# A hand-ordered attention and maxout kernel: another order of the same units, nine evictions moved to ScalarE, one bias replaced by a mask product

## The chip, the cores and the metric

The kernel runs on one core of a Trainium2 chip. A core has TensorE (PE; its weight loads are listed as PEld), VectorE (DVE), ScalarE (ACT), GpSimd (POOL) and SyncE (SP), which issues DMA transfers. The engines run side by side; each works through its own instructions strictly in program order, and semaphores hold an instruction until its inputs are there and its output buffer is free. The metric is device time of one execution in microseconds (us).

## The reference

```python
def _attn_ref(q, k, v, n_global, n_local) -> np.ndarray:
    B, H, S, D = q.shape                      # 4, 8, 768, 64
    scale = 1.0 / np.sqrt(D)
    scores = scale * np.matmul(q, k.transpose(0, 1, 3, 2))
    ...
    is_global = pos[None, :] < int(n_global)                # 8
    is_local = (rel >= 0) & (rel < int(n_local))            # 96
    keep = is_global | is_local
    dist = np.where(is_global & ~is_local, float(n_local), np.abs(rel).astype(np.float32))
    slopes = 2.0 ** (-8.0 * (np.arange(H, dtype=np.float32) + 1) / H)
    bias = -slopes[:, None, None] * dist[None, :, :]
    scores = np.where(keep, scores + bias[None], -1000000000.0)
    ...
    return np.matmul(softmax(scores), v)
def _moe_ref(x, w1, w2, w3, w_out) -> np.ndarray:           # x: 3072 x 512, d_ff = 768
    h = np.maximum(np.maximum(x @ w1, x @ w2), x @ w3)
    return (h @ w_out).astype(np.float32)
```

The last two lines of the first function are shortened to their meaning. The attention output, heads side by side, is x: 3072 rows of 512.

## The kernel before

The 3072 rows are 24 tiles T0 to T23 of 128 rows, six to a batch. A tile attends to itself, to the tile before it and to 8 global keys, which are copied over unused places of the tile before. The tiles are grouped in seven chunks (SIZES, line 89: 4, 2, 2, 4, 4, 4, 4 tiles) for the maxout product, which is computed transposed: chunk c, slice f of 128 of the 768 hidden features, matrix j of three.

Nothing is scheduled by a tool: the string SCHEDULE (line 25) lists 782 units in one order, and each engine gets its instructions in that order. A unit is a letter, numbers, sometimes a last number that chooses the engine that does it (0 ScalarE, 1 VectorE, 2 GpSimd) and, behind @, the buffer slot that it writes. For x, F, O, t, S, A and b that slot is one of the eight banks of PSUM (S, b and A take two neighbouring ones), so a unit with @4 on TensorE waits until the last user of bank 4 has been read out. The units that matter here:

| unit | what it does | line |
|---|---|---|
| l, w, q | load of queries, keys, values (l0, l1, l2; 512 KB for two tiles), weights, output weights, from SP's queue | 229, 236, 514, 523 |
| c, v, W, Q | casts to bfloat16: queries and keys (c0, c1 . pair of tiles), values (v tile . half), weights (W group . matrix), output weights | 195/201, 254 |
| x, y, X | transposes of queries and keys on TensorE with a copy out of PSUM, or as a DMA transpose (X) | 270/276, 283/287, 292 |
| G, V | copies of the global keys and of the global rows of the values | 313/315, 323/325 |
| b, S | bias added to a score tile by an identity matmul; the scores (S tile . half . 1 on top of a bias, 0 alone) | 335, 349 |
| e, m | exp on ScalarE; product with the mask of distances, needed only where no bias was added | 356, 365/367 |
| B, K | the bias and the mask, per head, made once at the start | 373, 378 |
| A, n | product with the values; division by the sum, into xb | 391/394, 402/403 |
| t, u, Z | transpose of xb to xT on TensorE with a copy, or as a DMA transpose (Z) | 418, 421, 424 |
| F, f | maxout product F c.f.j; f ...0 copies the first matrix's tile out of PSUM, f ...1 and f ...2 are maxes with the next two | 433, 447/449/452 |
| O, o, s | output product of one row tile; its copy; its store | 457, 471, 478 |
| E | the output products of the last three tiles of the last chunk but one piece | 457, 462, 463 |
| D | matmuls on zeros at the start | 532 |

Chunks 0, 1 and 2 and tile 11 get xT by t and u; the other tiles by Z. A cast by GpSimd (line 201) is two instructions, one by ScalarE or VectorE (line 195) one.

```python
    def u_c(slot, a, G, p, how):
        ...
        cast(how, dst, raw[a, G, p].rearrange("i (j s) (e d) -> i j e s d", s=2, e=2))
    def u_m(slot, T, g, how):
        if biased[T, g]:
            return
    ...
        for u in todo[:2] + [None] + todo[2:]:
            if u is None:
                setup()
                continue
            code, _, slot = u.partition("@")
            units[code[0]](int(slot) if slot else None, *(int(n) for n in code[1:].split(".") if n))
```

Of the kernel before, what the change touches and what calls it, by code (L numbers as in the profile page):

```python
# [34 lines left out]
    F0.2.0@5 f0.4.0.1@1 F0.1.0@6 v4.1.2 v4.0.2 l2.3.2@0 f0.1.0.0@2 q2@0 v5.1.0 F0.0.0@0 F0.5.1@1 F0.4.1@4  # L35
    F0.2.1@6 m4.0.1 f0.0.0.0@3 v5.0.0 f0.5.0.0@4 m5.1.1 A4@2 V4.1.0 F0.3.1@0 W0.1.2 f0.4.1.1 W0.2.0 m5.0.1
    f0.5.1.1 F0.0.1@1 F0.1.1@4 V4.0.1 W1.2.0 n4@1 t4@7 A5@2 W2.2.0 c1.3.2.2@0 f0.0.1.1 f0.1.1.1 F0.1.2@1
    n5@0 u4.1@1 f0.1.2.1@0 F0.0.2@4 q0@1 t5@7 u5.0 q1@2 f0.3.1.1 f0.0.2.1 F0.2.2@2 F0.3.2@3 f0.3.2.1
    c0.3.2.0 f0.2.0.0@2 f0.2.1.1 F1.2.0@4 F1.0.2@7 Q2.0 v7.1.2 F1.0.0@5 f1.0.0.1@3 v6.1.2 F1.0.1@3 f0.2.2.1
    f1.0.1.1 f1.2.0.1@0 Q0.2 f1.0.2.1@1 x3.1.2@6 y3.1.2.1@3 F0.4.2@5 f0.4.2.1 l1.4.2@3 v6.0.2 Q1.2 F1.1.0@0  # L40
    F1.2.2@1 l0.4.2@4 l1.6.2@5 F1.2.1@4 f1.2.1.1 F1.3.1@2 f1.2.2.1 F1.3.2@3 v7.0.2 F1.3.0@4 f1.3.0.0@2
    f1.3.1.1 f1.3.2.1 x3.0.2@1 F0.5.2@5 f0.5.2.1 F1.4.0@2 F1.1.1@3 f1.1.0.0@3 y3.0.2.0 S6.0.0@0 S6.1.0@4
    G6.2 c1.4.2.2@1 c0.4.2.2 l0.5.2@0 c0.5.2.2@2 f1.1.1.1 f1.4.0.0@1 e6.0@4 S7.0.0@6 S7.1.0@2 l1.5.2@6
    c1.5.2.2 e6.1@5 c1.6.2.2@0 e7.1@6 F1.4.1@0 e7.0@7 l2.4.2@1 O0.2@1 f1.4.1.1 m7.1.1 x4.1.2@0 F1.5.2@2
    F1.5.0@3 m7.0.1 v8.1.2 F1.5.1@4 A7@6 f1.5.0.1@0 m6.1.1 m6.0.1 o0.2.0@0 y4.1.2.0@0 f1.5.1.1 f1.5.2.1
    x4.0.2@3 y4.0.2.0 G7.0 l0.6.2@1 c0.6.2.2 F1.4.2@5 O0.1@4 f1.4.2.1 n7@2 o0.1.1@1 A6@0 l2.5.2@2 S8.1.0@2
    S8.0.0@6 n6@3 V7.1.1 G8.1 v8.0.2 F1.1.2@4 O0.3@5 t6@0 v11.0.2 v9.0.2 v9.1.2 f1.1.2.1 V7.0.0 t7@1 e8.1@0
# [564 lines left out]
```

## Time and profile before

| | us |
|---|---|
| median of 3 runs | 175.62 (174.99 to 176.35) |
| the profiled execution | 176.69 |
| its span, first to last instruction | 174.8 |
| DMA: bytes moved, mean rate | 37.36 MB, 214 GB/s |

One execution was recorded by the hardware profiler. A busy time is the time in which an engine had at least one instruction under way. "Idle before" is the time that an engine stood still before an instruction, with what released it. The chain of waits is followed back from the last instruction: at each step to what released it, or to the instruction before it on its engine. PEclk is the clock that TensorE was granted, 1.00 being full.

### The profile page before, as it was taken

To read this page: it belongs to the slowest core of one execution; us is meant where nothing else is said; L and a number is where in the kernel's file an instruction comes from. 1 tells how busy PE (TensorE), PEld (TensorE's weight loads), DVE (VectorE), ACT (ScalarE), POOL (GpSimd) and SP (SyncE) were. 2 spreads that over 40 slices of the span, in tenths; PEclk is the share of its full clock that TensorE was granted. 3 is DMA by queue.
4 is the path that set the end of the run, shared out by engine and by line. 5 is a ranking of instruction groups with operands and counts; after the bars stand their busy time and mean duration, and the time that the engine had idled before them with its cause. 6 is when DMAs were issued, how large, how long until landed. Compare 5 with 4: busy or idle time off the path is not lost.

```text
span 174.8 us, 3865 instructions
## 1 busy us (share of the span) xinstructions
PE 165.9 (95%) x1485; PEld 93.6 (54%) x1507; DVE 131.9 (75%) x268; ACT 95.4 (55%) x147; POOL 54.7 (31%) x99
## 2 busy tenths in 40 slices
PE   7997999999999999898999999999999999999991
PEld 2555745577676877544445545544445554444460
DVE  7889864988599897989898678899578993074910
ACT  5988897672868788440667688200345651402051
POOL 4049295057586717003730003240530000000000
PEclk9999999999999999999999999999999999999998
DMA  5999999999899899999996759998990046370035
GB/s 149 352 292 327 402 360 385 270 371 311 229 303 179 139 183 266 267 290 284 165 135 112 114 145 306 305 210 260 231 213 20 0 120 137 121 286 4 0 119 185
DMA packets 66403, 37.36 MB, mean 214 GB/s; under 512 B 24144, under 2 KB 61392, under 8 KB 66384
## 3 DMA queue, kind: packets, MB, share of 16 engines
q1 hardware_dynamic: 66240, 37.04, 83.3%
q8 instruction: 12, 0.20, 0.5%
q10 hardware_dynamic: 144, 0.07, 0.1%
q14 instruction: 7, 0.06, 0.1%
HBM read 25.17 MB, written 6.29 MB: 180 GB/s over the span
## 4 chain that ended last, share of the span: by engine, by line
PE 76%; DVE 10%; DMA 6%; ACT 3%; issue 2%; SPq 0%; DVEq 0%
PE psum L433 44%; PE psum L457 17%; PE psum L349 6%; DMA xT<-xb 3%; DMA rawqk<-in_k_dram 3%; DVE P L365 3%; PE psum L391 3%; PE psum L394 2%; PE psum L276 2%; DVE ht L452 1%; DVE xb L403 1%; ACT P L356 1%; PE psum L270 1%; DVE qb L195 1%; PE psum L335 1%
## 5 line engine op out<-in xcount | busy, mean ns | idle before, releaser
L433 PE MATMUL psum<-xT,w 128*128 128x512 bf16 (+1 forms) x491 | 97.5, 348 | 1.5 <-DMA xT<-xb 0.7
L433 PEld LDWEIGHTS <-w 128*128 128x128 bf16 x504 | 47.6, 98 | 42.9 <-DMA xT<-xb 0.9
L356 ACT ACTIVATE P<-psum 128x1024 bf16<-128x1024 f32 (+1 forms) x48 | 43.3, 954 | 10.4 <-PE psum L349 10.3
L449 DVE TENSOR_TENSOR h<-h,psum 128x512 bf16<-128x512 bf16 (+1 forms) x42 | 25.0, 605 | 15.9 <-PE psum L433 12.4
L457 PE MATMUL psum<-wo,ht 128*128 128x512 bf16 (+2 forms) x147 | 33.4, 362 | 0.5
L447 ACT CAST h<-psum 128x512 bf16<-128x512 f32 (+1 forms) x27 | 13.8, 523 | 33.1 <-PE psum L433 29.8
L452 DVE TENSOR_TENSOR ht<-h,psum 128x512 bf16<-128x512 bf16 (+1 forms) x42 | 26.2, 644 | 2.1 <-PE psum L433 0.9
L365 DVE TENSOR_TENSOR P<-P,wmask 128x1024 bf16<-128x1024 bf16 x34 | 25.2, 752 | 2.0 <-ACT P L356 1.7
L457 PEld LDWEIGHTS <-ht 128*128 128x128 bf16 x156 | 13.8, 98 | 13.5 <-DVE ht L452 0.2
L254 POOL CAST va<-rawv 64x512 bf16<-64x512 f32 x28 | 18.5, 668 | 4.8 <-DMA rawv<-in_v_dram 3.7
L323 POOL COPY va<-vaf 4x260 int32<-4x260 int32 x17 | 7.2, 424 | 34.9 <-PE psum L394 34.5
L403 DVE TENSOR_TENSOR xb<-psum,rz 128x512 bf16<-128x512 f32 x24 | 16.6, 692 | 0.8
L201 POOL CAST qb<-rawk 128x512 bf16<-128x512 f32 x12 | 7.5, 654 | 23.7 <-DMA rawk<-in_k_dram 23.7
L349 PE MATMUL psum<-qkT 64*128 64x128 bf16 x352 | 14.4, 217 | 0.5 <-DVE qkT L315 0.4
L391 PEld LDWEIGHTS <-P 128*128 128x128 bf16 x192 | 12.6, 97 | 3.2 <-ACT P L356 0.4
L349 PEld LDWEIGHTS <-qkT 64*128 64x128 bf16 x352 | 10.0, 94 | 7.9 <-issue 5.9
L391 PE MATMUL psum<-va,P 128*128 128x65 bf16 x160 | 12.7, 193 | 0.7 <-DVE ht L452 0.6
L447 DVE CAST h<-psum 128x512 bf16<-128x512 f32 (+1 forms) x15 | 9.1, 615 | 5.1 <-PE psum L433 5.1
L471 ACT COPY staging<-psum 128x512 f32<-128x512 f32 x14 | 8.2, 592 | 8.8 <-PE psum L457 8.8
L201 POOL CAST qb<-rawq 128x512 bf16<-128x512 f32 x14 | 8.9, 664 | 9.0 <-DMA rawq<-in_q_dram 5.0
L394 PEld LDWEIGHTS <-P 128*128 128x128 bf16 x160 | 10.5, 97 | 2.1 <-issue 0.7
L394 PE MATMUL psum<-va,P 128*128 128x65 bf16 x128 | 9.9, 193 | 0.0
(72 smaller groups left out, 120.6 us busy)
## 6 DMA issues: line engine op xcount, KB each, us to landing
rawv<-in_v_dram SPq DMA_DIRECT2D x12, 512.0 KB, 7.0
out_dram<-staging SPq DMA_DIRECT2D x21, 256.0 KB, 2.7
rawq<-in_q_dram SPq DMA_DIRECT2D x10, 512.0 KB, 7.1
rawk<-in_k_dram SPq DMA_DIRECT2D x10, 512.0 KB, 7.3
staging<-in_moe_w_dram SPq DMA_DIRECT2D x3, 1024.0 KB, 9.3
staging<-in_moe_w_dram SPq DMA_DIRECT2D x3, 512.0 KB, 8.8
staging<-in_moe_w_out_dram SPq DMA_DIRECT2D x3, 512.0 KB, 6.3
out_dram<-staging SPq DMA_DIRECT2D x5, 128.0 KB, 2.2
```

Source lines behind the costliest of these rows:

```text
L254: copies[how](heads(va(T))[64 * e:64 * e + 64, :, 0:D], src)
L349: nc.tensor.matmul(sp[:, hh, j2, ds], qT(T - ds, 1, hsl, jp), qT(T, 0, hsl, jp), start=not how, stop=True, skip_group_check=True)
L356: nc.scalar.activation(P[:, :, 0:n], sps[T, g].rearrange("p a b d n -> p (a b) d n")[:, :, 0:n], AF.Exp, bias=0.0, scale=scale)
L365: mul(P, P, wmask[:, g, :, 0:2])
L391: nc.tensor.matmul(o, P[:, i, 0], heads(va(T))[:, h], start=True, stop=(t == 0), skip_group_check=True)
L394: nc.tensor.matmul(o, P[:, i, 1], heads(va(T - 1))[:, h], start=False, stop=True, skip_group_check=True)
L403: nc.vector.tensor_tensor(out=x.rearrange("p (g h) d -> p g h d", g=2), in0=o4[:, :, :, 0:64], in1=rz[:, :, :, None].to_broadcast([128, 2, ...
L433: nc.tensor.matmul(ps, w123[f // 2][:, j, dm, (f % 2) * 128:(f % 2) * 128 + 128], xT[c][:, dm], start=(dm == 0), stop=(dm == 3))
L447: copies[how](h01, ps)
L449: nc.vector.tensor_max(h01s[c, f], h01s[c, f], ps)
L452: nc.vector.tensor_max(dst, h01s[c, f].rearrange("p (t e i) -> p t e i", e=2, i=64), ps.rearrange("p (t e i) -> p t e i", e=2, i=64))
L457: nc.tensor.matmul(po, ht[c][:, f, tt * 128:(tt + 1) * 128], wo[:, f, cols], start=(f == 0), stop=(f == NF - 1))
```

## The change

SCHEDULE gets another order of the same units, but for one: the unit b1.0 (bias for the first half of T1's heads) goes, S1.0 starts its scores alone, and m1.0, a mask product on VectorE, comes in. Engines change for about ninety units; counted over the whole kernel, evictions f ...0, q/k casts, value copies, row copies and bias scalings gain 3, 4, 6, 5 and 2 on ScalarE, which gives up two weight casts, one cast of output weights, three key copies, two xT copies and one output copy; VectorE gains three weight casts, one of output weights, two xT copies, one output copy and the mask product, and gives up 6 value copies, 5 row copies, 3 evictions, 2 bias scalings, 2 key copies and 1 q/k cast; GpSimd gains 5 key copies and gives up 3 q/k casts and one weight cast. The order of the loads on SP's queue differs: l0.12.3 and l1.12.3 change places at the start, l2.3 comes ahead of l1.3 and l0.3, l1.4 ahead of the output weights, and l1.7, l1.8, l1.9 ahead of l0.9. Slots change throughout; so do the banks and stages of the last unit. No function is changed.

```diff
SCHEDULE = """
-    l0.12.1@0 l1.12.1@1 D10.512@0 l1.12.3@2 l0.12.2@3 l0.12.3@4 R K7 K6 B1.1 K4 B2.1 K2 B3.0 K1 K5 B0.1 B6.1
-    K0 c0.12.3.2@0 l1.12.2@5 c0.12.1.1 B4.1 B5.1 c1.12.1.1@1 K3 x12.0.1@0 y0.0.1.0@0 B7.1 l2.0.2@0 D3.256@1
-    x12.1.1@1 b0.1@2 v1.0.2 l2.1.2@1 c1.12.3.1 v1.1.2 b1.0@4 y0.1.1.0 b1.1@6 S1.1.1 l0.2.2@6 c0.12.2.1
...
-    V1.1.1 V1.0.2 G2.1 v3.1.2 w0.2@2 A0@2 S3.0.1 e3.0@6 b3.1@6 n1@0 c0.2.2.2@2 S3.1.1 G3.0 A2@0 V2.0.2
-    e3.1@7 V2.1.2 n0@1 t0@2 W0.0.2 c1.2.2.1 u0.0@0 x2.1.2@3 y2.1.2.0@2 w1.2@2 x2.0.2@2 A3@4 t1@6 u1.0 n2@2
-    y2.0.2.1 t2@7 n3@3 l0.3.2@1 l1.3.2@2 S4.1.0@0 V3.1.2 e4.1@0 V3.0.2 S4.0.0@2 W1.1.2 u2.1 t3@6 G4.1 u3.0
-    W2.0.1 S5.1.0@4 e5.1@2 S5.0.0@0 e5.0@1 m4.1.1 W1.0.1 e4.0@3 F0.5.0@7 F0.4.0@6 W2.1.0 F0.3.0@4 f0.3.0.0@0
...
-    x4.0.2@3 y4.0.2.0 G7.0 l0.6.2@1 c0.6.2.2 F1.4.2@5 O0.1@4 f1.4.2.1 n7@2 o0.1.1@1 A6@0 l2.5.2@2 S8.1.0@2
...
-    m10.1.1 e11.0@0 f2.0.0.0@1 A10@2 V10.0.2 f2.1.1.1 m11.1.1 o1.0.0@4 n10@3 Z8@0 V10.1.0 l0.7.2@2 v11.1.2
-    v15.1.2 v12.1.2 F2.5.2@0 O1.1@1 v12.0.2 S12.1.0@2 e12.1@3 S13.1.0@4 m11.0.1 Z9 f2.5.2.1 S13.0.0@6
-    o1.1.1@5 F2.4.2@0 A11@2 n11@2 F2.0.1@1 e13.1@1 F2.3.1@4 m12.0.1 m12.1.1 e13.0@2 c0.7.2.1@1 Z10 f2.0.1.1
...
-    A12@2 n12@1 f2.3.2.1 f3.1.0.1@2 F3.1.1@1 f3.1.1.1 v13.0.1 l1.9.2@0 c1.9.2.1 F3.0.2@0 F3.0.1@5 f3.0.1.1
-    F3.1.2@4 f3.0.2.1@1 F3.2.0@1 F3.2.2@2 l1.7.2@6 c1.7.2.2 f3.1.2.1 F3.5.0@3 A13@4 V13.1.1 f3.5.0.1@3 n13@0
...
-    f4.3.0.0@0 v20.0.2 G18.0 F4.1.2@1 f4.1.0.1@3 c0.11.2.2@1 m17.0.1 v17.0.1 l2.11.2@2 n16@3 s3.1 f4.5.0.0@4
-    V16.0.2 m19.0.1 l0.10.2@3 F4.0.1@0 F4.1.1@7 m19.1.1 f4.4.0.0@1 F4.5.2@6 c0.10.2.2@2 A19@2 Z16 n19@1 Z19
...
+    l0.12.1@0 l1.12.1@1 l0.12.3@2 l0.12.2@3 R B0.1 B5.1 B6.1 l1.12.2@4 K1 D10.512@0 B4.1 B7.0 K0 B2.0
+    l1.12.3@5 K2 l2.0.2@0 K6 b0.1@0 c0.12.1.1@0 c1.12.1.1@1 B1.0 x12.0.1@2 y0.0.1.1@0 x12.1.1@3 c0.12.3.2 K3
+    K4 B3.1 b1.1@4 x12.0.3@6 c0.12.2.1 l2.1.2@1 c1.12.2.2 v1.1.2 y0.1.1.0 y1.0.1.0@1 y1.1.1.1 v1.0.2
...
+    e1.0@3 e2.1@4 v0.1.1 e2.0@5 b3.0@0 A0@4 l1.2.2@0 v2.0.2 S3.0.1 e3.0@6 m1.0.1 A1@2 c0.2.2.0@2 n0@0 n1@1
+    w1.0@0 b3.1@6 v3.0.2 t0@4 w0.0@0 S3.1.1 e3.1@7 V1.1.1 t1@5 V1.0.1 w1.1@1 c1.2.2.1 u1.1@0 v2.1.2 A2@0
+    V2.1.2 V2.0.2 x2.0.2@2 y2.0.2.0@2 l2.2.2@2 n2@2 K7 w0.1@1 x2.1.2@3 y2.1.2.1 G3.2 u0.0 w0.2@2 A3@6 n3@3
+    t2@2 S4.1.0@0 e4.1@1 u2.1 S4.0.0@4 V3.1.2 W2.0.1 G4.2 t3@3 u3.0 v4.0.2 w1.2@2 K5 W1.0.1 S5.1.0@6
+    S5.0.0@0 v4.1.2 l2.3.2@0 e4.0@2 W0.0.1 m4.1.1 V3.0.1 e5.0@0 m5.0.1 m4.0.1 F0.4.0@2 l1.3.2@1 l0.3.2@2
...
+    f1.1.0.0@2 f1.4.0.0@3 f1.2.1.1 F1.3.2@2 f0.5.2.1 Q1.2 f1.3.1.1 f1.3.2.1 F1.2.2@3 S6.0.0@0 f1.2.2.1
+    e6.0@4 l0.5.2@5 l1.5.2@6 S7.1.0@4 S7.0.0@6 S6.1.0@2 e6.1@5 e7.0@6 F1.5.0@0 F1.5.1@1 x4.1.2@2 F1.1.1@3
...
+    o0.1.0@1 e8.1@1 V7.0.0 e8.0@2 A6@2 c1.6.2.2@0 v8.0.2 c0.6.2.0 t7@0 n6@3 O0.3@1 t6@2 F1.1.2@3 v9.1.2
+    u7.1@2 v9.0.2 S9.1.0@6 S9.0.0@4 e9.1@0 m8.1.1 e9.0@3 u6.1 G9.0 m8.0.1 o0.3.1@2 F2.5.0@0 O0.0@2
...
+    f2.2.2.1@0 V9.1.2 F2.5.2@1 F2.3.0@2 e11.1@5 m11.1.1 F2.0.0@3 e11.0@1 A10@4 f2.5.2.1 l2.6.2@0 O1.1@0
+    n10@2 f2.0.0.0@2 f2.3.0.0@0 V10.0.0 m11.0.1 S12.1.0@2 e12.1@2 S13.0.0@4 V10.1.2 o1.1.1@5 S13.1.0@6
+    F2.4.2@1 A11@2 l2.7.2@1 v14.0.2 v14.1.2 Z8@0 Z9 Z10 v12.0.2 v12.1.2 e13.1@0 l1.7.2@3 e13.0@3 F2.0.2@0
...
+    c1.8.2.2@1 F2.1.2@4 f2.1.2.1 l1.9.2@5 c0.7.2.0@2 v15.0.0 l0.9.2@6 v13.1.0 F3.1.0@2 m13.0.1 c1.7.2.2
+    f3.1.0.0@1 F3.0.1@3 F3.0.0@1 f3.0.0.0@3 A12@4 n12@0 F3.4.0@2 F3.0.2@1 v13.0.0 f3.4.0.1@4 F3.2.1@7 A13@4
+    V13.0.0 f2.3.2.1 F3.1.1@2 F3.1.2@6 c1.9.2.2@0 f2.0.2.1 f3.0.1.1 f3.0.2.1@1 F3.2.0@3 V13.1.0 F3.4.1@0
...
+    F4.2.1@4 F4.5.0@5 l0.10.2@1 m19.0.1 v19.1.2 A19@2 F4.3.2@6 f4.5.0.0@1 F4.2.0@5 o3.1.0@11 V15.1.0 m16.0.1
...
+    S20.1.0@4 c0.11.2.0 e20.0@2 F4.0.2@6 f4.0.2.1 F5.5.1@1 e20.1@4 G20.0 F5.3.1@7 S21.1.0@2 e21.1@0 v22.1.2
...
-LAST_BANKS = (6, 7, 3, 0, 1, 4, 5, 2)
...
-LAST_STAGES = (8, 2, 0, 10, 11, 7, 6, 3, 4, 9, 1, 5)
+LAST_BANKS = (7, 3, 6, 5, 0, 4, 1, 2)
...
+LAST_STAGES = (7, 6, 4, 8, 2, 1, 11, 9, 5, 3, 0, 10)
```

More of the change, by code (lines that the diff above doesn't have):

```diff
@@ L35 @@
[L35 to L39, printed above, removed]
@@ new lines @@
+    v17.1.0 F4.3.0@1 m17.0.1 m17.1.1 l1.10.2@2 l1.11.2@4 l2.10.2@1 F4.0.1@7 n19@0 V19.0.0 f4.2.0.0@0
+    f4.3.0.0@3 v16.1.2 A16@2 V16.0.2 f4.2.1.1 V16.1.2 F4.4.1@1 F4.1.0@4 n16@2 f4.1.0.1@4 v17.0.0 A17@2
+    F4.4.0@5 c1.11.2.0@2 F4.1.2@4 n17@3 l2.11.2@2 v22.0.2 F4.4.2@2 s3.3 Z19@2 f4.4.0.0@2 v21.1.2 c1.10.2.2@0
+    f4.4.1.1 f4.4.2.1@0 F4.5.1@1 Z18 v20.0.2 v21.0.2 s3.1 F4.1.1@3 f4.1.1.1 f4.1.2.1 f4.5.1.1 F4.3.1@2
+    F4.5.2@5 s0.2 Z16 f4.2.2.1 f4.3.1.1 f4.3.2.1 Z17 F5.0.0@3 F5.2.0@1 v20.1.2 c0.10.2.2 G19.2 f5.2.0.0@2
@@ new lines @@
+    V20.1.2 O4.1@6 G22.1 m22.0.1 e22.1@6 A21@0 n21@1 F5.1.1@7 S23.0.0@2 e23.0@5 V21.1.2 v23.1.2 o4.1.0@11
+    S23.1.0@0 V21.0.2 F5.3.2@4 m22.1.1 f5.3.2.1 F5.4.1@5 F5.5.2@6 e23.1@7 A22@0 m23.0.1 O4.2@4 V22.0.2
+    V22.1.0 f5.4.1.1 m23.1.1 f5.1.1.1 A23@2 F5.4.2@5 n22@2 f5.5.2.1 F5.1.2@0 n23@3 Z20@0 f5.4.2.1 s2.1
+    O4.3@1 s1.0 s0.0 Z21 Z22 o4.3.0@0 f5.1.2.1 O5.1@0 o5.1.0@5 Z23 O5.3@1 o5.3.1@8 F6.1.0@0 F6.1.1@5
+    o4.2.0@4 f6.1.0.0@2 F6.5.0@4 F6.1.2@0 F6.2.1@1 F6.4.1@2 s4.0 F6.0.0@3 s2.0 F6.0.2@6 f6.5.0.0@1
@@ L87 @@
+    f6.0.0.0@0 F6.0.1@3 F6.5.1@4 f6.1.1.1 s4.2 f6.0.1.1 F6.3.2@5 F6.4.0@3 f6.4.0.0@4 s5.3 s0.3 f6.1.2.1@0
+    s0.1 F6.3.0@0 F6.4.2@3 f6.3.0.0@3 s3.2 s4.1 s3.0 s5.1 f6.4.1.1 f6.4.2.1 f6.0.2.1 F6.2.0@0 f6.2.0.0@2
+    f6.2.1.1 F6.3.1@2 f6.3.1.1 f6.3.2.1 F6.2.2@0 F6.5.2@1 f6.2.2.1 O5.2@2 f6.5.1.1 o5.2.0@3 f6.5.2.1 s5.2
+    s4.3.2 E@1 O5.0@2 o5.0.0@10 s5.0.2
 """
```

71 lines of the change are left out of this document (29 added, 42 removed).

## The prediction

> **What bounds the kernel now.** I read the engine totals first, then busy time by stage, then the chain of waits, then the groups of instructions, then single stretches of the timeline.
>
> ```profile
> PE 165.9 (95%) x1485; PEld 93.6 (54%) x1507; DVE 131.9 (75%) x268; ACT 95.4 (55%) x147; POOL 54.7 (31%) x99
> ```
> ```profile
> core 0: us, PE busy (x) PEld busy (x) DVE busy (x) ACT busy (x) POOL busy (x), PEclk, DMA share, GB/s
> 0.00:21.40 21.40, 18.78 (x235) 11.06 (x235) 18.17 (x54) 17.78 (x30) 9.12 (x22) 1.00 1.01 302
> 21.40:47.00 25.60, 25.30 (x208) 15.60 (x209) 18.46 (x35) 17.55 (x26) 15.36 (x25) 1.00 1.05 326
> 47.00:73.00 26.00, 25.13 (x327) 18.63 (x329) 22.91 (x51) 19.91 (x32) 13.69 (x22) 1.00 1.07 219
> 73.00:91.00 18.00, 17.20 (x125) 8.43 (x126) 15.96 (x30) 6.92 (x9) 6.13 (x10) 1.00 1.12 229
> 91.00:117.00 26.00, 25.67 (x244) 13.47 (x243) 21.03 (x40) 15.42 (x24) 5.83 (x11) 1.00 0.90 196
> 117.00:149.00 32.00, 31.73 (x251) 15.89 (x255) 25.06 (x47) 12.15 (x17) 4.56 (x9) 1.00 0.59 146
> 149.00:171.00 22.00, 21.89 (x113) 10.51 (x113) 10.31 (x16) 5.12 (x10) 0.00 (x0) 1.00 0.29 108
> ```
> TensorE bounds it. The stages are cut where the code changes pace: up to the first tile of the maxout product at 21.4 us, then chunks 0 and 1, chunk 2, chunk 3, and so on. After 21.4 us TensorE stands still for only 0.30 + 0.87 + 0.80 + 0.33 + 0.27 + 0.11 = 2.68 us. The diff leaves TensorE's work alone but for one bias, so 2.7 us, and whatever the first 21.4 us and the tail give, is the most that a new order can win; there is no such floor on the other side. VectorE has 3.2 us free before 21.4, 7.1 us in the next stage, 3.1 us from 47 to 73 and 2.0 us from 73 to 91: it is the engine that can become the bound.
>
> The chain of waits says where those 2.68 us and the start go (start, duration, what):
>
> ```profile
> 20.03 0.99 ACT P L356
> 21.02 0.52 ACT xT L421
> ...
> 67.78 4.98 DMA xT<-xb
> ...
> 79.51 0.43 DVE va L254
> ...
> 79.97 1.13 DVE qb L195
> 81.10 0.61 DVE h L449
> 81.73 1.34 DVE ht L452 x2
> ...
> 83.12 0.19 PE psum L391
> ```
> At the start ScalarE ends last: an exp, then the copy of T3's transpose, which the first tile of chunk 0 waits for. At 72.8 us it is Z10, a DMA transpose of 4.98 us. At 83.1 us A13 waits for VectorE, which works off a cast and two value copies ahead of the maxes that A13 stands behind.
>
> **The change, part by part.** Counting the units of both orders up to the same point gives what moves: TensorE's stages follow each other as before, with tiles swapped inside them; what differs is who evicts and casts. Durations (the number behind the comma is the mean of one in ns):
>
> ```profile
> L335 PE MATMUL psum<-bias,identb 128*128 128x512 bf16 x12 | 3.4, 381 | 0.1
> L195 DVE CAST w<-staging 128x1024 bf16<-128x1024 f32 x2 | 1.4, 686 | 0.0
> L195 ACT CAST qb<-rawq 128x1024 bf16<-128x1024 f32 x2 | 2.1, 1046 | 0.1
> L365 DVE TENSOR_TENSOR P<-P,wmask 128x1024 bf16<-128x1024 bf16 x34 | 25.2, 752 | 2.0 <-ACT P L356 1.7
> L325 DVE COPY va<-vaf 4x520 bf16<-4x520 bf16 x11 | 4.2, 381 | 0.9 <-PE psum L394 0.8
> L421 DVE COPY xT<-psum 128x512 bf16<-128x512 bf16 x3 | 1.2, 412 | 0.0
> L447 DVE CAST h<-psum 128x512 bf16<-128x512 f32 x11 | 7.5, 686 | 4.9 <-PE psum L433 4.8
> L373 DVE TENSOR_SCALAR bias<-rbase 128x384 bf16<-128x384 f32 x7 | 2.1, 355 | 0.0
> L378 ACT ACTIVATE wmask<-rbase 128x384 bf16<-128x384 f32 x8 | 3.5, 509 | 1.3 <-DVE rbase L565 1.3
> ```
> *VectorE, up to the first tile of chunk 3.* It gains three casts of weights and one of the output weights (4 x 0.686 = 2.74), two of the row copies (2 x 0.381 = 0.76), two xT copies (0.82), one mask product (0.75, of m1.0), one eviction (0.69) and one output copy of like size (0.69), and loses two bias scalings (0.71) and one copy of global keys (about 0.2): +5.5 us. Against that stand 3.2 + 7.1 + 3.1 = 13.4 us of free time in the same stretch, so the sum fits, with 7.9 us to spare. By the first tile of chunk 4 only about +0.6 us is left (the four casts 2.74 and the xT copies 0.82 against two bias scalings 0.71, two key copies 0.3, one q/k cast 0.69 and three value copies of some 0.42 each, 1.27): so VectorE does about 5 us less between those two points than before. That is the stage from 73 to 91.
>
> *Chunk 3 (73 to 91 us): -0.5.* The pieces ahead of A13 in the chain, v13.0 (0.43) and c1.9 (1.13), and v13.1 before them, leave VectorE: the v13 go to ScalarE, which is busy 6.92 of 18 us there, and c1.9 to GpSimd, 6.13 of 18. In the new order VectorE has only n12, one eviction and short maxes between A12 and A13. What is late next is v13.0 on ScalarE, queued behind c0.7 (1.05), two value copies and two evictions (about 0.6 each); counted on from the copy of T11's transpose, near 71.9, with the second eviction waiting for its tile, it ends near 76 us and A13 comes near 77.7. Of the 0.80 us of idle TensorE this can win all or nothing; I take 0.5, the wait before A13 less the step that any change from F to A costs.
>
> *Z10 at the head of chunk 3: 0.* n10 still follows A10 at once on VectorE, behind one max, and Z8, Z9, Z10 stay in that order on SP's queue; the query load that stood between Z8 and Z9 is now ahead of Z8. The row of TensorE's wait:
> ```profile
> 72.81 1.47 PE L433 MATMUL psum<-xT,w 128*128 128x512 bf16 x5 [0.66 <-DMA xT<-xb]
> ```
> Between A10 and the first tile of chunk 3 stand two matmuls of 512 columns fewer than before, some 0.4 us; so the wait may grow to 1.1 us, while the tile behind it is reached no later. Bounds -0.4 to +0.5; I take 0.
>
> *The cast that held a mask product: -0.3.*
> ```profile
> 108.19 2.86 DVE L365 TENSOR_TENSOR P<-P,wmask 128x1024 bf16<-128x1024 bf16 x2
> ```
> ```profile
> 108.28 2.79 DVE P L365 x2
> ...
> 111.11 0.20 PE psum L391
> ```
> ```profile
> 108.54 1.16 POOL L201 CAST qb<-rawq 128x512 bf16<-128x512 f32 x2
> ```
> Two mask products, of T19, took 2.86 us where two of 0.75 take 1.5; GpSimd's cast c0.11 ran meanwhile, and A19 waited for them until 111.1. In the new order c0.11 is on ScalarE and stands behind the first tiles of chunk 5, and only one value copy of GpSimd is left beside T19's products. Of the 0.33 us that TensorE stood still from 91 to 117 it can win all or nothing; as this is the one wait of length there, I take 0.3. The Trainium skill ("SBUF — State Buffer", section "SBUF: two separate sides") states that VectorE and GpSimd share one port pair as an exclusive lock for a whole instruction, when the VectorE operation has two SBUF inputs or runs in a 2-port mode. The trace agrees in this row. By that rule the casts of weights now on VectorE are exposed too; what this would give is the second rival's sum.
>
> *The start: -0.2.* ScalarE gets c0.2 (1.05) and one of the eight wmask exponentials (0.51) into the run before u3 and gives u1 (0.58) to VectorE: +0.98, against two waits for TensorE in that run:
> ```profile
> 15.35 1.02 ACT L356 ACTIVATE P<-psum 128x1024 bf16<-128x1024 f32 x1 [0.49 <-PE psum L349]
> 19.47 0.58 ACT L421 COPY xT<-psum 128x512 bf16<-128x512 bf16 x1 [0.47 <-PE psum L418]
> ```
> The 0.96 us of waits cover nearly all of it. For it, one qkT copy less, of about u1's size, stands before the first exp, and one bias of two passes (at most 2 x 0.381) goes from TensorE for a product that VectorE has time for. If the cover is gone and neither helps: +1.0; if all is covered and both help: -0.7. I take -0.2, a little on the side of the shorter queue in front of the first exp, because every later exp stands behind that one.
>
> *Heads of chunks 1 and 2, near 45 us: +0.2.* S6.1 now takes the banks of the tile evicted just before it (F1.2.2), and two F tiles stand behind the exp of S6.0. Both are short waits, 0 to 0.6.
>
> Everything else (14 value, key and row copies that change engine) lies beside TensorE's work, on ScalarE and GpSimd, which have at least 6 us free in each stage of the table from 21.4 us on. The tail after chunk 6 is the same but for one output tile put before the last step: 0.
>
> Sum: -0.2 + 0.2 + 0 - 0.5 - 0.3 = -0.8 us. The profiled execution took 176.69 us (span 174.8, 1.9 around it), so its like would be 175.9; it lay 1.07 above the median of the three runs, and the median goes from 175.62 to **174.8 us**.
>
> **The rivals.**
> *All idle time goes.* If the new order leaves no wait after 21.4 us, 2.7 us are won: 172.9. For it: the waits at 72.8, 83.1 and 111.1 all have a changed surrounding. Against: TensorE already runs 95%, and Z10's 4.98 us stays.
>
> *VectorE turns into the bound from 22 to 73 us (slower).* Its free time in chunks 0 and 1 (7.1 us of 25.6) shrinks by up to 4.8 (three weight casts 2.06, two evictions 1.37, two value copies 0.84, three row copies 1.14, an xT copy and a product 1.16, less 1.73 for scalings, key copies and a cast), and it now takes W0.0 just when that load lands:
> ```profile
> 21.75 1.67 POOL L201 CAST w<-staging 128x512 bf16<-128x512 f32 x2 [3.20 <-DMA staging<-in_moe_w_dram]
> ```
> Before, GpSimd bore that wait of 3.20 us; now the mask products of T4 and T5 and every max of chunk 0 are queued behind it. I count VectorE at most some 0.5 us ahead of TensorE near 37 us (chunk 0's last maxes), so it decides once VectorE falls behind by more than 0.5; slower than before once by more than 1.3. Three products held as at 108.19 (3 x 1.3 = 3.9, less 0.5 and less the 0.8 won) would give +2.6: 178.2; two give +1.3: 176.9. Middle 177.6. For it: the row of 108.19. Against: GpSimd has three casts of q/k and one of weights fewer.
>
> *Late loads* are a smaller cause of the same sign: six q/k casts go to ScalarE, whose exps are then queued behind a transfer.
> ```profile
> 53.84 1.23 POOL L201 CAST qb<-rawq 128x512 bf16<-128x512 f32 x2 [0.59 <-DMA rawq<-in_q_dram]
> ```
> c0.6 landed at 53.84; by my count ScalarE reaches it near 54.6, so it has 0.8 us.
>
> *It does nothing.* The moves lie off TensorE's path and new short waits take the place of old ones: 175.6.
>
> **How the numbers follow.** Forecast case (173.9 to 175.2) 0.32; nothing (175.2 to 176.4) 0.25; all idle time gone (172.5 to 173.8) 0.20; slower by VectorE or loads 0.23 (176.5 to 178.5). The range that leaves out half of the first extreme and a third of the last is 173.0 to 177.6. One per cent, 1.76 us, is about what a measurement of this kernel tells from no change (its three runs span 1.36 us). Faster by more: the case of no idle time and a little of the forecast's, 0.23. Slower by more (over 177.4): most of the slow case, 0.20. Within: 0.57.
>
> **What would show it.** Right: the wait before A13 gone, VectorE at 95% or less from 21 to 47 us, TensorE's idle time from 73 to 91 us below 0.4, a first chunk-0 tile near 21.2 us. Wrong: TensorE waiting for a max or a weight cast on VectorE between 25 and 60 us; a first tile later than 22; an exp waiting behind a cast that waits for a DMA.

## The result, and the profile after

The changed kernel takes 176.59 us (median; 176.25 to 177.39), the kernel before, run beside it, 175.95 (174.99 to 176.40). The ratio is 1.0041, with a 95% interval from 1.0025 to 1.0058: 0.64 us slower, where 0.8 us faster was forecast.

The profiled execution took 177.39 us, its span 175.5. The page's busy times:

```profile
PE 166.4 (95%) x1505; PEld 92.8 (53%) x1505; DVE 127.8 (73%) x257; ACT 103.7 (59%) x158; POOL 49.4 (28%) x96
```
As the diff promised, ScalarE works more (95.4 to 103.7) and VectorE less over the whole kernel (131.9 to 127.8). (Of the evictions f ...0, eleven go from VectorE to ScalarE and eight the other way: three on balance, not the nine of the title.) Line numbers shift with the length of SCHEDULE: in the changed kernel they are one higher than in the table of units, in the kernels of the experiments e1 to e10 four lower. The view by stages, cut as before (busy times of TensorE, its weight loads, VectorE, ScalarE, GpSimd):

```profile
core 0: us, PE busy (x) PEld busy (x) DVE busy (x) ACT busy (x) POOL busy (x), PEclk, DMA share, GB/s
...
21.40:47.00 25.60, 24.86 (x206) 14.86 (x203) 23.52 (x44) 13.90 (x23) 8.30 (x12) 1.00 1.05 326
...
73.00:91.00 18.00, 18.00 (x132) 8.68 (x131) 13.43 (x26) 10.00 (x16) 5.61 (x12) 1.00 1.26 240
91.00:117.00 26.00, 25.25 (x239) 13.29 (x238) 16.82 (x33) 18.26 (x28) 6.58 (x13) 1.00 0.99 204
```
In chunk 3 (73 to 91) TensorE is now busy throughout: 18.00, where it was 17.20. Not all of these 0.80 us were idle time: the first profile of the kernel before holds 1485 matmuls for 1507 weight loads, so 22 records are missing, three of them in this stage. In chunks 0 and 1 (21.4 to 47) VectorE goes from 18.46 to 23.52, and TensorE, which stood still for 0.30 us there, now does so for 0.74; from 91 to 117 its 0.33 become 0.75. What happens in the first of these stages is in the chain of waits (start, duration, what):

```profile
21.83 1.94 ACT P L357 x2
...
23.80 1.29 DVE P L366 x2
25.09 1.20 DVE w L196 x2
26.29 1.01 DVE P L366
...
27.34 0.73 DVE va L255
...
28.10 1.30 DVE h L448 x2
...
31.41 0.56 DVE va L326
...
31.98 0.60 DVE va L326
32.59 0.43 DVE va L255
33.02 0.12 DVE rz L403
...
33.16 0.70 DVE xb L404
...
33.91 0.40 PE psum L419 x4
```
From 23.8 to 33.9 us the chain runs on VectorE: mask products of T5 and T4, the casts of weights 2.1 and 1.1, a mask product, a value copy, evictions and maxes, the row copies V4.1 and V4.0, v5.0, and then the division of T4, which TensorE's transpose t4 waits for. In the kernel before the chain did not touch VectorE here:

```profile
22.01 7.50 PE psum L433 x34
...
30.26 2.32 PE psum L433 x10
32.59 0.22 PE psum L418 x4
```
TensorE's row of t4 in the changed kernel, with its wait:

```profile
33.91 0.40 PE L419 MATMUL psum<-identb,xb 128*128 128x128 bf16 x4 [0.48 <-DVE xb L404]
```
How much VectorE had to do up to this division is read from two windows, the first in the kernel before (T4's division starts at 30.70 there), the second in the changed kernel (at 32.93):

```profile
20.50:30.70 10.20, 9.88 (x74) 4.99 (x74) 6.31 (x13) 8.67 (x13) 6.96 (x10) 1.00 1.09 377
```
```profile
20.50:32.95 12.45, 12.37 (x90) 6.27 (x88) 11.76 (x21) 7.93 (x11) 4.54 (x7) 1.00 1.10 363
```
VectorE worked 6.31 us and stood idle for 3.89 before; it works 11.76 us now. 5.45 us more work is due before the division, and 3.89 us were free. Before, nearly all of that free time lay in two waits of VectorE for a tile of TensorE:

```profile
23.58 0.69 DVE L447 CAST h<-psum 128x512 bf16<-128x512 f32 x1 [1.18 <-PE psum L433]
...
28.69 0.69 DVE L449 TENSOR_TENSOR h<-h,psum 128x512 bf16<-128x512 bf16 x1 [2.65 <-PE psum L433]
```

Waits are also taken from the starts of the matmuls: the time from one start to the next, less what the earlier matmul takes itself (0.22 us for 512 columns, by the starts of an undisturbed run of them). By this measure TensorE loses 0.64 us ahead of t4 and 0.35 us ahead of two tiles of chunks 1 and 0 at 39.46 and 40.07, which take the banks of tiles that VectorE's maxes at 38.07 have to read first:

```profile
38.07 1.95 DVE L453 TENSOR_TENSOR ht<-h,psum 128x512 bf16<-128x512 bf16 x3
```
In the second execution of the changed kernel (a2 below) it loses 0.42 ahead of t4, 0.30 ahead of a tile at 31.94 that waits for a max, and 0.34 at the two tiles. Both come to 1.0 to 1.1 us, and the kernel before has none of these waits.

Where the time goes over the whole kernel is seen by comparing the moments at which TensorE had done the same amount of work, counted in the columns that its matmuls stream. The table is worked out from the starts of all matmuls in each recorded execution; entries are us later (+) or earlier (-) than the first recorded execution of the kernel before. Beside the first two profiles it takes further executions of both kernels, and two of the experiments below. The changed kernel does its tiles in another order, so that an entry of it can be off by some 0.2 us, the one at 126.5 by 0.4.

| work that before had done at | 31.5 | 48.4 | 70.4 | 92.8 | 109.7 | 126.5 | 147.7 | 168.1 |
|---|---|---|---|---|---|---|---|---|
| changed, first | -0.01 | +1.01 | +1.17 | -0.49 | +0.76 | +0.81 | +0.61 | +0.62 |
| changed, second | +0.13 | +1.17 | +1.33 | -0.21 | +0.28 | -0.03 | -0.22 | -0.22 |
| before, second | +0.16 | +0.16 | +0.64 | -0.17 | -0.15 | -0.02 | -0.01 | 0.00 |
| before, third | +0.04 | +0.04 | +0.04 | -0.83 | -0.82 | -1.11 | -1.10 | -1.10 |
| e3, no GpSimd casts beside VectorE | -0.13 | +0.30 | +0.43 | -1.31 | -0.70 | -0.63 | -0.82 | -0.82 |
| e5, four copies on ScalarE | -0.07 | -0.15 | -0.04 | -1.79 | -1.30 | -1.42 | -1.62 | -1.61 |

Two things stand out. Both executions of the changed kernel lose 1.0 us between 31.5 and 48.4 and win 1.5 to 1.7 between 70.4 and 92.8, in chunk 3 and its head. But the second and third execution of the kernel before win 0.8 and 0.9 there too, against the first one, without any change. Executions of one and the same kernel differ by up to 1.1 us, in steps that lie after 48 us, so no single profile is a base to a tenth.

### The profile page after: what moved, and what is told of

Its sections match the earlier page's. It is cut to its first block, busy times and chain, and to the rows that moved or that the text cites. A ratio compares the mean times of both kernels' runs of the same rounds, so it can differ in the third digit from the quotient of the medians.

```text
span 175.5 us, 3865 instructions
## 1 busy us (share of the span) xinstructions
PE 166.4 (95%) x1505; PEld 92.8 (53%) x1505; DVE 127.8 (73%) x257; ACT 103.7 (59%) x158; POOL 49.4 (28%) x96
## 4 chain that ended last, share of the span: by engine, by line
PE 75%; DVE 7%; DMA 7%; ACT 7%; issue 1%; POOL 1%; SPq 0%; POOLq 0%; DVEq 0%; ACTq 0%
PE psum L434 46%; PE psum L458 16%; PE psum L350 5%; ACT P L357 4%; PE psum L392 3%; DMA rawqk<-in_k_dram 3%; PE psum L395 3%; DMA xT<-xb 2%; DMA out_dram<-staging 2%; PE psum L277 1%; DVE P L366 1%; ACT qkT L284 1%; DVE h L450 1%; DVE va L326 1%; PE psum L419 1%
## 5 line engine op out<-in xcount | busy, mean ns | idle before, releaser
L434 PE MATMUL psum<-xT,w 128*128 128x512 bf16 (+1 forms) x504 | 99.2, 349 | 1.2 <-ACT P L357 0.9
L448 ACT CAST h<-psum 128x512 bf16<-128x512 f32 (+1 forms) x30 | 15.2, 525 | 27.4 <-PE psum L434 27.0
L366 DVE TENSOR_TENSOR P<-P,wmask 128x1024 bf16<-128x1024 bf16 x35 | 23.8, 707 | 1.9 <-ACT P L357 1.9
L255 POOL CAST va<-rawv 64x512 bf16<-64x512 f32 x30 | 19.5, 651 | 15.3 <-DMA rawv<-in_v_dram 12.6
L472 ACT COPY staging<-psum 128x512 f32<-128x512 f32 x13 | 7.5, 586 | 9.3 <-PE psum L458 8.2
L448 DVE CAST h<-psum 128x512 bf16<-128x512 f32 (+1 forms) x12 | 7.3, 619 | 2.3 <-PE psum L434 2.3
L202 POOL CAST qb<-rawk 128x512 bf16<-128x512 f32 x12 | 6.9, 609 | 7.5 <-DVE h L448 5.0
L403 DVE RECIPROCAL rz<-psum 128x8 f32<-128x8 f32 x24 | 4.8, 201 | 4.9 <-PE psum L392 2.0
```

Of the source, the lines that this page charges most:

```text
L255: copies[how](heads(va(T))[64 * e:64 * e + 64, :, 0:D], src)
L366: mul(P, P, wmask[:, g, :, 0:2])
L434: nc.tensor.matmul(ps, w123[f // 2][:, j, dm, (f % 2) * 128:(f % 2) * 128 + 128], xT[c][:, dm], start=(dm == 0), stop=(dm == 3))
L448: copies[how](h01, ps)
```

## The experiments

Theory W: VectorE has more work before 33 us than it has time, and T4's division comes late. Rival L: not the work, but GpSimd's casts beside it, which stretch VectorE's short copies. Rival S: the heads of chunks 4 and 5, through the order of SP's queue. Each timed ratio below is against the kernel before, run on the same chip in the same session; the changed kernel's own is 1.0041. Where a run is said to lie above or below the changed kernel, that is the difference of the two ratios, times 176 us. With intervals of about 0.2% on each ratio, such a difference is known to some 0.5 us.

**e1: three weight casts back.**
```diff
- W0.0.1 ... W1.1.1 ... W2.1.1
+ W0.0.2 ... W1.1.2 ... W2.1.0
```


> Changed kernel with three of the weight casts where they were before: the casts of weights 0.0 and 1.1 by GpSimd, 2.1 by ScalarE. It takes 1.8 us of work from VectorE between 21 and 26 us, and gives GpSimd some 4 us of casts in the same stretch. Theory W (VectorE has too much work before 33 us, so that the division of tile 4 ends at 33.85 and TensorE waits 0.86 us for it): the division ends 1 us or more earlier, the wait at 32 to 41 us falls by 0.6 to 0.9, the time is 0.5 to 0.9 us below the changed kernel. Rival L (VectorE is late because GpSimd's instructions stretch its short copies, 1.1 us instead of 0.7 and the like): more work on GpSimd gives more of it, the division ends no earlier and the time is the same or up to 0.5 us longer. Rival S (TensorE's loss at the heads of chunks 4 and 5, from the order of SP's queue, decides alone): no change beyond 0.2 us.

Measured: 180.58 us (four executions, 178.4 to 182.5), ratio 1.0212 (1.0141 to 1.0283): 3.0 us above the changed kernel, which no theory had. GpSimd's timeline (start, duration, line, what; idle time before it and what ended it) and the list of TensorE's waits from 20 to 47 us (in total, times, longest):

```profile
25.84 1.28 POOL L250 CAST va<-rawv 64x512 bf16<-64x512 f32 x2 [5.12 <-DMA rawv<-in_v_dram]
27.18 5.29 POOL L197 CAST w<-staging 128x512 bf16<-128x512 f32 x8
```
```profile
PE psum L429 <- POOL w L197: 3.1, 2, 2.7
```
In the order of the changed kernel GpSimd's next unit is a value cast that waits 5.12 us for its load. The weight casts behind it begin at 27.18, and the next tiles of chunk 0 wait for them. The edit was a bad test of W: it put work on an engine whose queue stood still. A second cost followed. TensorE had been idle for 2.7 us, and from 29.05 to 32.46 the clock granted to it was 0.50, which the stage shows as 0.93:

```profile
21.40:47.00 25.60, 22.23 (x149) 11.88 (x151) 19.09 (x35) 11.02 (x18) 10.30 (x17) 0.93 1.06 327
```
In these 3.4 us matmuls of 512 columns started 0.43 us apart instead of 0.22, some 1.7 us in all. So the 3.0 us are not the wait alone: the one execution of e1 with a mean clock of 1.00 took 178.4, the others, at 0.99, 180.6 to 182.5.

**e2: four value copies to ScalarE.**
```diff
- v5.1.1 ... W1.2.0 ... v7.0.0 V4.1.1 V4.0.1 v5.0.1
+ v5.1.0 ... v7.0.0 V4.1.0 V4.0.0 W1.2.0 v5.0.0
```


> Changed kernel with four short value copies (V4.1, V4.0, v5.1, v5.0) moved from VectorE to ScalarE, and the weight cast W1.2.0 on ScalarE put behind them. VectorE loses 2.3 us of busy time between 27 and 33 us, weight casts and GpSimd stay as they are. Theory W: the division of tile 4 ends near 31.6 instead of 33.85, TensorE's wait at 32 to 34 us (0.86) goes, the time is 0.7 to 1.0 us below the changed kernel. Rival L: the same, since the copies were the instructions that were stretched; this run does not tell W and L apart, the others do. Rival T (the wait would come anyway, from the tile's exponentials or the values' product): the division stays at 33.5 or later and less than 0.2 us is gained.

Measured: 179.47 us, ratio 1.0188 (1.0126 to 1.0250), 2.6 us above the changed kernel. ScalarE's timeline:

```profile
32.80 0.62 ACT L250 CAST va<-rawv 64x512 bf16<-64x512 f32 x1 [3.34 <-DMA rawv<-in_v_dram]
33.43 1.26 ACT L321 COPY va<-vaf 4x520 bf16<-4x520 bf16 x2
34.59 1.04 ACT L191 CAST w<-staging 128x1024 bf16<-128x1024 f32 x1
35.64 0.62 ACT L250 CAST va<-rawv 64x512 bf16<-64x512 f32 x1
```
The same trap: v7.0 waits 3.34 us for its load, and the copies moved behind it come at 33.4 to 36.3. Tile 5's product waited 2.7 us for them, and here too the granted clock was 0.50 for 3.4 us from 35.8 on, which is part of the 2.6 us. The half of the test that W speaks of did come out: with the copies gone T4's division ended at 31.3 instead of 33.85, and t4 did not wait.

**e3: no GpSimd casts beside VectorE's copies.**
```diff
- W0.2.0 ... W0.1.2 ... W2.2.2
+ W0.1.0 W0.2.0 ... W2.2.0
```


> Changed kernel with the two weight casts that GpSimd does at 25 to 33 us (0.1 and 2.2) given to ScalarE. VectorE keeps every instruction. Rival L: V4.1 and V4.0 take 0.28 us each instead of 0.55 and 0.60 and the instructions before them shrink too, together 0.6 to 1.2 us, and the wait at 32 to 34 us falls by as much; the time is 0.4 to 0.9 us below the changed kernel. Theory W: the copies shrink by no more than 0.5 us together, TensorE still waits 0.5 us or more for the division, and ScalarE's two further casts (some 0.6 us each) push its exponentials: the time is within 0.4 us of the changed kernel or above it.

Measured: 175.99 us, ratio 1.0004 (0.9985 to 1.0023): 0.37% below the changed kernel's ratio, 0.65 us. GpSimd in the changed kernel, then VectorE in this experiment (timelines):

```profile
27.85 1.25 POOL L202 CAST w<-staging 128x512 bf16<-128x512 f32 x2
31.20 1.23 POOL L202 CAST w<-staging 128x512 bf16<-128x512 f32 x2 [2.11 <-DMA staging<-in_moe_w_dram]
```
```profile
31.29 0.58 DVE L321 COPY va<-vaf 4x520 bf16<-4x520 bf16 x2
31.89 0.42 DVE L250 CAST va<-rawv 64x512 bf16<-64x512 f32 x1
32.23 0.20 DVE L398 RECIPROCAL rz<-psum 128x8 f32<-128x8 f32 x1
32.46 0.69 DVE L399 TENSOR_TENSOR xb<-psum,rz 128x512 bf16<-128x512 f32 x1
```
The row copies V4.1 and V4.0 take 0.58 us together where the chain above shows 0.56 and 0.60, and the division ends at 33.15 instead of 33.85. In the table the loss up to 48.4 falls from 1.01 to 0.30; by the starts of the matmuls t4 no longer waits, while the 0.35 us at the two tiles near 40 us stay. So L has a part of 0.65 us, within its expected range. In the changed kernel the two copies end at 32.58, 0.15 us behind the second half of GpSimd's cast (31.20 + 1.23 = 32.43): they take turns with its halves. The Trainium skill ("SBUF — State Buffer", section "SBUF: two separate sides") says that a VectorE operation in a 2-port mode and a GpSimd instruction hold their common ports in turn, each for its whole length; this row agrees. The two evictions at 28.10, which read PSUM, stood beside GpSimd's cast at 27.85 and took their usual 0.69 each. Which instruction is caught differs between executions: in the second one of the changed kernel V4.1 takes 0.53 and V4.0 0.28, but a weight cast beside the cast v4.0 takes 1.11 instead of 0.68.

**e4: SP's queue.**
```diff
- Z13@1 ... X17 ... Z12 ... Z14 ... Z18 ... s3.1 ... s0.2 Z16 ... Z17
+ Z13@1 Z12 ... X17 ... Z14 ... Z18 ... Z16 ... Z17 s3.1 s0.2
```


> Changed kernel with another order on SP's queue alone: Z12 goes right behind Z13 (its input, the division of tile 12, is there at 77 us, and it now goes out behind X17 at 96.7), and the stores s3.1 and s0.2 go behind Z17. No compute instruction is moved. Rival S: Z14 and Z15 end some 1.0 to 1.6 us earlier and the wait of TensorE at the head of chunk 4 (102 to 103 us, 0.95 lost against the kernel before) goes nearly whole; at the head of chunk 5 (118 us) 0.3 to 0.5 us are gained; the time is 0.8 to 1.4 us below the changed kernel. Theory W alone: the two heads gain, but what is gained there is lost again later or was not on the path, and the time moves by less than 0.3 us. Rival D (the transfers themselves, not the place in the queue, are late): Z15 ends within 0.3 us of where it does now, no gain at either head.

Measured: 176.28 us, ratio 1.0021 (1.0000 to 1.0042). That is 0.2%, 0.35 us, below the changed kernel, but the two intervals overlap. By the spans of the two profiles (175.5 and 174.4) it looked like 1.1 us. The wait at the head of chunk 4 in the first profile of the changed kernel, on the weight loads of TensorE:

```profile
102.95 2.29 PEld L434 LDWEIGHTS <-w 128*128 128x128 bf16 x12 [0.90 <-DMA xT<-xb]
```
It is not in e4. To see whether e4 took it away or whether it comes and goes, both kernels were recorded again.

**a2 and b2: both kernels again, unchanged.**

> The changed kernel once more, for a second profile: its first recorded execution took 177.39 us, 0.8 above its median, while the recorded ones of the third and fourth experiment lie at their medians. By that pair of profiles the queue experiment gained 1.0 us at the heads of chunks 4 and 5, by the medians 0.3. If the waits at those two heads vary from execution to execution, this profile shows them smaller than 0.95 and 0.56 us and the profile's 1.0 was too large; if they are as long as before, the 0.8 lies elsewhere (at the start or spread over all) and the queue experiment's gain is 1.0 less something that it lost elsewhere.

> The kernel before once more, for a second profile: its first recorded execution took 176.69, 0.9 above the median of the later runs. If the difference lies in waits of single stages, those rows of the first profile were too long and the sum made from them too; if it is spread or lies at the start or the end, the rows of the stages stand.

The changed kernel took 176.45 us, span 174.6; there is no wait at either head. SP's queue in the first execution, then in the second (the last three transposes for chunk 4, Z12, Z14 and Z15):

```profile
96.76 4.83 SPq L425 DMA_TRANSPOSE xT<-xb  x3
```
```profile
95.07 4.31 SPq L425 DMA_TRANSPOSE xT<-xb  x3
```
The same queue ran 1.7 us ahead without any edit, so most of what e4's profile seemed to gain can be the difference between two executions. The kernel before took 176.60; b3 below completes it. In this second execution the wait of chunk 3's first tile for Z10 (0.66 us) is absent, and a wait near 64 us stands in its place; tile 13's product waits as it did:

```profile
82.85 0.19 PE L391 MATMUL psum<-va,P 128*128 128x65 bf16 x1 [0.51 <-DVE ht L452]
```

**e5: the copies on ScalarE, ahead of what waits for loads.**
```diff
- v5.1.1 ... W1.2.0 ... v7.0.0 V4.1.1 V4.0.1 v5.0.1
+ v5.1.0 ... V4.1.0 V4.0.0 v5.0.0 W1.2.0 v7.0.0
```


> As the second experiment (four value copies V4.1, V4.0, v5.1, v5.0 from VectorE to ScalarE), but on ScalarE the cast v7.0, which waits for its load until 32.8 us, and the weight cast W1.2 now come behind the copies; in that experiment the copies stood behind v7.0 and TensorE waited 3.2 us for tile 5's values. Theory W (VectorE has too much work before 33 us): the division of tile 4 ends at 31.5 or earlier instead of 33.85, TensorE waits less than 0.2 us at 32 to 34 us and the time is 0.5 to 1.0 us below the changed kernel. Rival H (ScalarE's own order, not VectorE's work, now sets the stage: the copies and W1.2 late behind one another): TensorE waits 0.3 us or more for tile 5's values or for a tile with matrix 1.2, and the gain is under 0.4 us.

Measured: 175.64 us, ratio 0.9980 (0.9958 to 1.0002): 0.61%, 1.07 us, below the changed kernel. The chain of waits over the same stretch:

```profile
21.93 7.50 PE psum L429 x34
...
30.19 3.19 PE psum L429 x14
33.37 0.22 PE psum L414 x4
```
VectorE is gone from it; TensorE alone carries it. The division ended at 31.3, and in the table the stretch up to 48.4 gives -0.15 where the change gives +1.01; by the starts of the matmuls neither t4 nor the two tiles near 40 us wait. Weight casts, GpSimd and everything else are those of the changed kernel. W holds: 0.95 us by the medians and 1.07 by the ratios, for the 0.5 to 1.0 expected. The copies taken away are also those that GpSimd's casts stretched, so e5 by itself does not tell W from L; e3 does that.

**e6: e3 and e4 together.**

> Changed kernel with the edits of the third and fourth experiment together (weight casts 0.1 and 2.2 from GpSimd to ScalarE; Z12 ahead, two stores back on SP's queue). They touch stages far apart, so if each gain reaches the end they add: 0.6 and 0.3 us as measured, 0.9 us below the changed kernel, 175.7, level with the kernel before or 0.2 us faster. Rival (the stages are coupled, so that an earlier start of chunk 3 finds its transfers late): the gain is no larger than that of the third experiment alone, 175.9 to 176.1.

Measured: 175.80 us, ratio 0.9984 (0.9964 to 1.0004). 0.57% below the changed kernel is the sum of 0.37 and 0.20, as expected if the two edits add. But 0.20% is no more than the interval of either ratio, so the rival is not excluded.

**e8: chunk 3's moves alone, in the kernel before.**
```diff
- v13.1.1 ... v13.0.1 ... c1.9.2.1
+ v13.1.0 ... v13.0.0 ... c1.9.2.2
```


> Kernel before with three of the change's moves in chunk 3 alone: the value copies v13.0 and v13.1 by ScalarE, the cast c1.9 by GpSimd. By the rows of the profile of before VectorE gets back 2.0 us there, the product of tile 13 no longer waits 0.77 us, and the time is 0.4 to 0.7 us below the kernel before. Rival R (these waits are of the recorded execution, and other executions, whose median is 0.7 below it, have less of them or give it back at the heads of chunks 4 and 5): 0 to 0.3 us.

Measured: 175.86 us, ratio 1.0000 (0.9981 to 1.0018). Rival R: nothing beyond 0.3 us either way, though A13 no longer waits in its profile. Its only wait in the list from 70 to 92 us is another:

```profile
PE psum L429 <- DVE ht L448: 0.3, 1, 0.3
```
It is that of a later tile of chunk 3, at 86.65, for a max on VectorE.

**b3: the kernel before against itself.**

> The kernel before compared with itself. Both of its recorded executions so far lie 0.6 to 0.9 us above the median of its unrecorded ones. If recording lengthens this kernel, its first run here is again near 176.6 and the ones behind it near 175.9, and the sum made from its rows starts 0.7 too high; if the two were chance, this profile lies near the median. The ratio is 1 within 0.002.

Measured: ratio 1.0006 (0.9986 to 1.0026), and the recorded execution took 175.63, its span 173.7. So recording does not lengthen it, and the first two were chance. Chunk 3 in this execution, by stages, and its first tile's wait:

```profile
73.00:91.00 18.00, 18.00 (x131) 8.65 (x130) 16.29 (x33) 7.74 (x10) 6.24 (x10) 1.00 1.15 226
```
```profile
72.51 2.33 PE L433 MATMUL psum<-xT,w 128*128 128x512 bf16 x10 [0.32 <-DMA xT<-xb]
```
TensorE is busy for all of 73 to 91, as in the changed kernel, where the first profile had 17.20. Z10's wait is 0.32 instead of 0.66, and by the starts of the matmuls A13 waits 0.11 instead of 0.54. The wait whose removal was priced at 0.5 us is a fifth as long in another execution of the same kernel, so that e8 had little to win.

**e10: the load on VectorE, put into the kernel before.**
```diff
- W0.0.2 ... W1.1.2 ... W2.0.1 ... W1.0.1 ... W2.1.0 ... f0.4.0.1@1 ... v5.1.0 ... v5.0.0 ... V4.1.0
+ W2.0.1 ... W1.0.1 W0.0.1 ... f0.4.0.1@1 W2.1.1 W1.1.1 ... v5.1.1 ... v5.0.1 ... V4.1.1
```


> Kernel before with the change's moves onto VectorE in chunk 0 alone: weight casts 0.0, 1.1 and 2.1 and the value copies V4.1, v5.1 and v5.0 by VectorE, the weight casts put behind VectorE's other work there. VectorE gets 3.2 us more between 21 and 31 us, where it stood idle for 4. Theory W: the division of tile 4 and the maxes behind it come 0.5 to 1.2 us later, TensorE waits for them between 27 and 40 us, and the time is 0.4 to 1.1 us above the kernel before. Rival P (only the order of the change does it, the work fits into the idle time): within 0.3 us.

Measured: 177.85 us, ratio 1.0110 (1.0075 to 1.0145): 1.9 us, more than W expected. VectorE, then TensorE (timelines):

```profile
30.24 0.29 DVE L321 COPY va<-vaf 4x520 bf16<-4x520 bf16 x1 [0.65 <-PE psum L390]
30.54 0.69 DVE L445 TENSOR_TENSOR h<-h,psum 128x512 bf16<-128x512 bf16 x1
31.14 0.68 DVE L361 TENSOR_TENSOR P<-P,wmask 128x1024 bf16<-128x1024 bf16 x1
31.75 0.68 DVE L445 TENSOR_TENSOR h<-h,psum 128x512 bf16<-128x512 bf16 x1
```
```profile
32.48 1.89 PE L429 MATMUL psum<-xT,w 128*128 128x512 bf16 x8 [1.45 <-DVE h L445]
```
The 4 us in which VectorE stood idle before did not take the 3.2 us. Part of it is the place: V4.1 waits for A4 until 30.24, and the maxes that free TensorE's banks are queued behind it; TensorE waits for such a max, not for T4's division. So the same moves, without the rest of the change, are enough to make the kernel slower; how much of the 1.9 us is load and how much is this place was not separated.

**e9: e5 and e4 together.**

> Changed kernel with the edits of the fifth experiment (four value copies on ScalarE ahead of the casts that wait for loads) and of the fourth (Z12 ahead, two stores back on SP's queue) together. If both gains reach the end: 0.95 and 0.3 us, 175.35, 0.3 to 0.4 per cent below the kernel before. Rival (coupled stages): no better than the fifth alone, 175.6.

Measured: 175.56 us, ratio 0.9977 (0.9960 to 0.9994). It is the one version whose whole interval lies below the kernel before. Against e5 (0.9980) the queue's edit adds nothing that can be told: e4's 0.35 us is either less than that or did not add here.

## Why the prediction was wrong

The range held the time, and so did the likeliest class, within 1%. The sign was wrong: the sum was -0.8 and the chip gave +0.64.

*The step that failed: VectorE up to the first tile of chunk 3, at no cost.* The prediction set 5.5 us of further work against 13.4 us of idle time and left VectorE out of the sum. Where the work went tells against it: VectorE's busy time grew by 5.1 us between 21.4 and 47, where it had 7.1 idle, and most of the new work (three weight casts of 0.68, v5.1 of 0.73, V4.1 of 0.56, v5.0 of 0.43, V3.0 of 0.28, one eviction and one max) stood ahead of T4's division, which TensorE needs at 33 us. Up to that division only 3.89 us were free, for 5.45 us more. The term should have been about +1.0: the table shows it in both recordings, the starts of the matmuls show it as waits for the division and for maxes, and e5 takes it away (1.07 us). e10, with these moves in the kernel before, is slower too (1.9 us), though there TensorE waits for a max behind V4.1. The second rival named the mechanism, VectorE too late in chunk 0. What it priced did not occur: W0.0 did not wait for its load (three weight casts ran from 20.61 in 1.91 us), and instead of three mask products held by 1.3 us each one was held, by 0.4. Its time, 177.6, was 1 us too high.

*The shared port.* The prediction cited the lock for one mask product and noted that the weight casts on VectorE were exposed. In the sum it had no term for chunk 0. There v5.1 took 0.73 us where v5.0 takes 0.43, and the two row copies 0.58 more than in e3. (The mask product ahead of them, 1.01 in the chain, was stretched in the kernel before too.) e3 returns 0.65 us of the 1.0, the wait of t4. The two causes are not rivals but parts: VectorE is late by the sum of both, and removing either takes away that wait; the 0.35 us near 40 us went only with the load. What v4.0 and v4.1 on GpSimd cost the instructions beside them was not tried by itself.

*Chunk 3, -0.5: right mechanism, price of one execution.* The wait before A13 is gone, as named, and TensorE is busy nearly throughout chunk 3 (18.00 of 18 us in the first profile, 17.81 in the second). But the price, 0.54 in the execution it was read from, was 0.46 and 0.11 in the others. In b3 the view by stages shows no idle time in those 18 us, and e8, the three moves alone, gave 0 with an interval of 0.3 us on either side. What else the changed kernel wins in this stretch was not tried. The 2.68 us of idle time that the prediction took as the most to be won are too many as well: they come from the profile that lacks 22 matmuls.

*A19, -0.3: right.* By the starts of the matmuls the kernel before waited 0.28 and 0.42 us inside A19 in two executions and not at all in the third; the changed kernel loses at most 0.06. So the 0.3 is there against two executions of three.

*The head of chunk 3, 0 within -0.4 to +0.5.* In the changed kernel's profiles the wait for Z10 is not among TensorE's waits; by the starts its first tile of chunk 3 loses 0.08 and 0.20. In the kernel before it is 0.66, none and 0.32 in three executions, so the gain is real in some and nothing in others.

*The start, -0.2.* The first weight load of chunk 0 came at 21.42, with 21.43 before, and its first matmul at 21.57, with 21.58 before: 0, and the sign "near 21.2" fell.

*The heads of chunks 1 and 2, +0.2.* The tile of chunk 1 behind the exp of S6.0 waited 0.16 at 46.45; S6.1 itself did not wait. Right, by the second of its two reasons.

*Everything else beside TensorE.* Not foreseen are the heads of chunks 4 and 5, where the first recorded execution waited 0.90 and, by the starts, 0.37 us, and the second not at all; the first of these waits was for a transpose, by its row. (The 0.56 us of an expectation above, like the 0.86 for t4 and the 0.77 for A13, still hold the 0.22 us of the matmul ahead.) By e4 the order of SP's queue is worth some 0.35 us, which its interval does not tell from nothing.

Counted by the means of the table's rows (two executions after, three before): +1.0 up to 48.4, -1.0 from 70.4 to 92.8 (chunk 3 together with its head, where -0.5 and 0 were forecast), and +0.6 behind that, all of it from the first execution's heads of chunks 4 and 5; together +0.57 at the end, against 0.64 in the medians. Only the first of the three parts is the same in both executions of the changed kernel. The other two rest on few executions, and e4, e8 and e9 do not settle them.

Of the signs named, the wait before A13, the idle time from 73 to 91 and the VectorE share (23.52 of 25.6, 92%) came out right and yet the time did not. The share is the instructive one: VectorE was at most 95% busy over the stage and still late in its first half. The decisive sign was the one listed as wrong: TensorE waiting for VectorE between 25 and 60 us, for the division and for maxes.

## What to carry to other kernels

An engine's idle time counts only before the moment at which its work is due: add up the moved work and the idle time up to the first instruction that TensorE waits for, not over the stage. Before giving an instruction to an engine, look at what stands ahead of it in that engine's own order: behind a cast that waits for a load, a few short instructions cost 3.0 and 2.6 us here (e1, e2; part of it through TensorE's clock, which was halved for 3.4 us after the wait), and the copies of e2 ahead of it won 1.07 (e5). And price a wait that a transfer releases from several executions, since it can be 0.7 us in one and nothing in the next. Check, too, whether a profile holds all matmuls before reading idle time off it.

## What was not expected of the hardware

Two recorded executions of one order differed by 1.1 us in span (174.8 and 173.7), in waits for a transfer (Z10, 0.66 and 0.32) and for VectorE (A13, 0.54 and 0.11; A19, 0.28 and none); the transposes on SP's queue that start at 96.76 in one execution of the changed kernel start at 95.07 in the other. And 4 x 520 row copies, which take 0.29 us alone, double to 0.56 and 0.60 beside a GpSimd cast, while evictions from PSUM of 0.69 us beside the same kind of cast do not change. After TensorE had stood idle for 2.7 us in e1 and e2, the clock granted to it was 0.50 for 3.41 us; after the wait of 1.45 us in e10 it stayed at 1.00.
